# Second-layer logits from seven block products over pairs of token tiles instead of eight

## Chip, core and metric

One core of a Trainium2 chip runs the whole program. The metric is the device time of one execution in microseconds (us); lower is better. TensorE (PE) multiplies matrices, VectorE (DVE), ScalarE (ACT) and GpSimd (POOL) do elementwise work, and SP here only issues transfers. Each engine takes its instructions in the order in which the program holds them.

## The reference

Windowed attention gives 2304 tokens of width 512, and two feed-forward layers follow. The second one is what matters here:

```python
def _moe2_ref(x, w_in, w_out, g_ln):      # x 2304x512, w_in 512x1024, w_out 1024x512
    h = x @ w_in
    h_max = np.max(h, axis=-1, keepdims=True)
    e = np.exp(h - h_max)
    sm = e / (np.sum(e, axis=-1, keepdims=True) + 1e-09)
    solu = h * sm
    mu = np.mean(solu, axis=-1, keepdims=True)
    var = np.mean((solu - mu) ** 2, axis=-1, keepdims=True)
    ln = (solu - mu) / np.sqrt(var + 1e-06) * g_ln
    return (ln @ w_out).astype(np.float32)
```

All data is float32. A float32 product is made of three fast ones: each operand is split into a rounded high part (type fp32r) and the rest, its low part, and high x high, high x low and low x high are added up in PSUM.

## The kernel before

The first part, up to about 523 us, runs attention and the first layer. The first layer goes through six blocks j of 384 tokens; in each block, 16 steps f make a hidden tile (`moe_h`, line 399) and, two steps later, add its product with `w_out` to four accumulators (`moe_y`, line 430). Attention of later tiles is fed in between in small slots. At a block's end `moe_out` copies the accumulators out and POOL sends them to DRAM (`x2d`). In the last block the second layer's weights are loaded, already split (`w2_load`, lines 210 to 217), into the buffers that the first layer's weights leave, and `x2_load`/`x2_split` (lines 549 to 563) load and split the first tokens.

The second layer takes 18 tiles of 128 tokens. For tile i:

- `st_h2` (line 645): 24 matmuls of 128x512 give the logits, 128x1024, in two PSUM banks; there are three such pairs of banks.
- `st_ln` (lines 656 to 668): DVE takes the row maximum, ACT the exponential into a tile `e`, DVE forms the normalised product `s`, ACT its squares, POOL the power -1/2, and DVE the scaled result. `e` and `s` have two buffers.
- `st_move` (lines 679 to 685): the result must be turned around for the next product. DVE transposes 32x32 blocks (into `e`), SP sends the tile to DRAM (`lnd`, one transfer of 512 KB), and, when it has landed, loads it back turned (`lT`, four transfers of 128 KB). The last three tiles (`DIRECT`) are turned on PE instead (line 698).
- `st_t2` (lines 703, 704): ACT makes the high part of `lT` and DVE the low part.
- `st_out` (lines 715 to 722): 24 matmuls of 128x512 give the output tile, ACT copies it, SP sends it to DRAM.

The loop at the end emits `st_h2(i)`, then `st_out(i - 4)`, then the normalisation of tile i, then `st_t2` of tile i - 3, which is pinned behind instructions of the current tile. A scheduler of the build then sets the final order on each engine from its own estimate of times; the order can be read from the built program, and the rows in the section on the change are from there.

Of the kernel before, what the change touches and what calls it, by code (L numbers as in the profile page):

```python
# [20 lines left out]
def kernel(  # L21
# [12 lines left out]
    nc = tc.nc  # L34
# [51 lines left out]
    ps_at = fr_ctx.enter_context(tc.tile_pool(name="ps_at", bufs=2, space=PSUM, side="right"))  # L86
    ps_h = fr_ctx.enter_context(tc.tile_pool(name="ps_h", bufs=2, space=PSUM, side="right"))
    ring = []
    ps_acc = ps_ctx.enter_context(tc.tile_pool(name="ps_acc", bufs=1, space=PSUM))
# [86 lines left out]
    w2ih, w2il, w2oh, w2ol = {}, {}, {}, {}  # L176
    w2d = [dram.tile([128, 1024], F32, name=f"w2d{u}") for u in range(16)]
# [257 lines left out]
    def moe_out(j, es):  # L435
        for e in es:
            xo = wk_p.tile([128, NB], F32, tag="xo", name="xo")
# [109 lines left out]
    x2h, x2l, x2raw = {}, {}, {}  # L547

    def x2_load(j):
        r = d_p.tile([128, KC, NB], F32, tag="x2", bufs=1, name="x2r")  # L550
        nc.sync.dma_start(out=r, in_=x2d[j].rearrange("e p n -> p e n"))
        x2raw[j] = r

    def x2_split(j, es):
        r = x2raw[j]
        if 0 in es:
            x2h[j] = wk_p.tile([128, KC, NB], F32R, tag="xh", name="x2h")
            x2l[j] = wk_p.tile([128, KC, NB], F32R, tag="xl", name="x2l")
        for e in es:
            nc.scalar.copy(x2h[j][:, e, :], r[:, e, :])  # L560
            nc.vector.tensor_tensor(
                x2l[j][:, e, :], r[:, e, :], as_f32(x2h[j][:, e, :]), op=ALU.subtract
            )

# [3 lines left out]
    for n in range(len(seq) + 2):  # L568
# [39 lines left out]
        if n < len(seq):  # L608
# [5 lines left out]
            if last and f >= 2 and f - 2 < 8:  # L614
                w2_load(f - 2, 0)
                w2_load(f - 2, 1)
# [4 lines left out]
        if n < len(seq):  # L621
            if last and 10 <= f < 14:
                x2_split(0, (f - 10,))
            if last and f == 14:
                x2_load(1)
# [4 lines left out]
    ps2 = ctx.enter_context(tc.tile_pool(name="ps2", bufs=2, space=PSUM, reuse_waits="tile"))  # L630
    h2, ln, lnh, lnl = {}, {}, {}, {}
    DIRECT = (NI - 3, NI - 2, NI - 1)
    lnd = [dram.tile([128, DF2], F32, name=f"lnd{i}") for i in range(NI)]

    def st_h2(i):
        j, t = divmod(i, TPN)
        ps = ps2.tile([128, DF2], F32, tag="h2", bufs=3, name="ps_h2")
        tc_ = slice(t * 128, t * 128 + 128)
        for nn in range(2):
            cs = slice(nn * 512, nn * 512 + 512)  # L640
            n = 0
            for kc in range(KC):
                hi, lo = x2h[j][:, kc, tc_], x2l[j][:, kc, tc_]
                for a, w in ((hi, w2ih), (hi, w2il), (lo, w2ih)):
                    nc.tensor.matmul(ps[:, cs], a, w[kc, nn], start=(n == 0), stop=(n == 3 * KC - 1))  # L645
                    n += 1
        h2[i] = ps

    def st_ln(i):
        ps = h2.pop(i)  # L650
        e = d_p.tile([128, DF2], F32, tag="e", name="e")
        s = d_p.tile([128, DF2], F32, tag="s", name="s")
        l_ = s
        st = d_p.tile([128, 8], F32, tag="stat", name="stat")
        nmx, sm, rs, ssum, nmu, vs, rstd = (st[:, z:z + 1] for z in range(7))
        nc.vector.reduce_max(nmx, ps, axis=mybir.AxisListType.X, negate=True)
        nc.scalar.activation(e, ps, ACTF.Exp, bias=nmx, scale=1.0, accum_out=sm)
        nc.vector.tensor_scalar(sm, sm, 1e-9, None, op0=ALU.add)
        nc.vector.reciprocal(rs, sm)  # L659
        nc.vector.scalar_tensor_tensor(s, ps, rs, e, op0=ALU.mult, op1=ALU.mult, accum_out=ssum)  # L660
        nc.vector.tensor_scalar(nmu, ssum, -1.0 / DF2, None, op0=ALU.mult)
        last_act = nc.scalar.activation(e, s, ACTF.Square, bias=nmu, scale=1.0, accum_out=vs).ins
        nc.vector.tensor_scalar(vs, vs, 1.0 / DF2, 1e-6, op0=ALU.mult, op1=ALU.add)
        nc.gpsimd.tensor_tensor(rstd, vs, mhalf, op=ALU.pow)
        if i in DIRECT:
            l_ = e.rearrange("p (k b i) -> p b k i", b=4, i=32)
            s = s.rearrange("p (b k i) -> p b k i", b=4, i=32)
        last_dve = nc.vector.tensor_scalar(l_, s, nmu, rstd, op0=ALU.add, op1=ALU.mult).ins
        ln[i] = l_, e
        return last_act, last_dve  # L670

    def st_move(i):
        l_, lt = ln[i]
        if i not in DIRECT:
            lT = d_p.tile([128, 4, NK2, 32], F32, tag="st", bufs=NST, name="lT")
            nc.vector.transpose(lt, l_)
            nc.sync.dma_start(out=lnd[i], in_=lt)  # L680
            for a in range(4):
                nc.sync.dma_start(
                    out=lT[:, a].rearrange("p k j -> p (k j)"),
                    in_=lnd[i][32 * a:32 * a + 32, :].rearrange("i (b m) -> b i m", b=4),
                )
            ln[i] = lT

    def st_t2(i):
        lnh[i], lnl[i] = {}, {}
        l_ = ln.pop(i)  # L690
        for a in range(2):
            hi, lo = wtile(f"wih{8 + 2 * (i % 2) + a}"), wtile(f"wil{8 + 2 * (i % 2) + a}")
            lnh[i][a], lnl[i][a] = (z.rearrange("p (k t) -> p k t", t=128) for z in (hi, lo))
            if i in DIRECT:
                if a == 0:
                    ps = ps2.tile([128, DF2], F32, tag="h2", bufs=3, name="ps_t2")
                    for c in range(0, DF2, 128):
                        nc.tensor.transpose(ps[:, c:c + 128], l_[1][:, c:c + 128], ident)
                src = ps[:, 512 * a:512 * a + 512]
            else:  # L700
                src = l_[:, :, 4 * a:4 * a + 4, :].rearrange("p a k j -> p k a j")
                hi, lo = (z.rearrange("p (k a j) -> p k a j", k=4, a=4) for z in (hi, lo))
            nc.scalar.copy(hi, src)
            nc.vector.tensor_tensor(lo, src, as_f32(hi), op=ALU.subtract)


    def st_out(i):
        hi, lo = lnh.pop(i), lnl.pop(i)
        w = DM // 2 if i == NI - 1 else DM
        for c in range(0, DM, w):  # L710
            ps = ps2.tile([128, DM], F32, tag="o", name="ps_o")[:, 0:w]
            n = 0
            for kk in range(NK2):
                for a, b in ((hi, w2oh), (hi, w2ol), (lo, w2oh)):
                    nc.tensor.matmul(  # L715
                        ps, a[kk // 4][:, kk % 4, :], b[kk][:, c:c + w],
                        start=(n == 0), stop=(n == 3 * NK2 - 1),
                    )
                    n += 1
            o = d_p.tile([128, DM], F32, tag="o", name="o")[:, 0:w]  # L720
            nc.scalar.copy(o, ps)
            nc.sync.dma_start(out=out[i * 128:(i + 1) * 128, c:c + w], in_=o)

# [4 lines left out]
    pins = []  # L728
    for i in range(NI + LAG):
        if i < NI:  # L730
            st_h2(i)
        if i >= LAG:
            st_out(i - LAG)
        if i - 2 in DIRECT:
            st_t2(i - 2)
        if i < NI:
# [42 lines left out]
```

## Time and profile before

| what | value |
|---|---|
| median of three runs | 736.18 us (734.31 to 736.62) |
| the profiled execution | 734.42 us, of which the span from first to last instruction is 732.6 us |
| mean granted clock of PE in it | 0.990 of full speed |
| busy: PE, DVE, ACT, POOL | 709.4, 416.9, 399.2, 142.3 us |
| first layer's last matmul begins | 522.92 us |
| second layer | from 523.26 us to the end |

A busy time adds up the instructions' own durations. Matmuls are pipelined, so the durations of neighbours overlap; how fast PE goes is read from the distance of the starts. The trace names the instruction that each engine waited for, and the SP queue's timeline shows when a transfer could be issued, which for `lT` is the moment when `lnd` has landed.

### The profile page before, as it was taken

Reading aid. Unit: us, or ns where it says so; the run is one execution under the profiler, and the core shown is the slowest. Engines: PE = TensorE matmul, PEld = TensorE weight load, DVE = VectorE, ACT = ScalarE, POOL = GpSimd, SP = SyncE. Lnnn points to the kernel's source line nnn. Section 1 sums busy time; section 2 is a strip of 40 time slices with the busy share of each in tenths; the row PEclk is TensorE's granted clock in tenths of the full one; section 3 lists DMA queues with packets and bytes.
Section 4 is the critical chain, followed back from the end, with each engine's and each line's share of the span. In section 5 each row is a group of like instructions: output and inputs, shape, how many; then the busy total and the mean of one; then the engine's idle time right before and its main releaser. Section 6 shows DMA issues by size and latency. Waiting matters only on the chain.

```text
span 732.6 us, 12336 instructions
## 1 busy us (share of the span) xinstructions
PE 709.4 (97%) x4321; PEld 649.4 (89%) x4321; DVE 416.9 (57%) x1110; ACT 399.2 (54%) x986; POOL 142.3 (19%) x167
## 2 busy tenths in 40 slices
PE   7799889999999999999999999999999899999998
PEld 5699779999999999999999999999887688888887
DVE  4669987655555665655565543322386547466550
ACT  5878867655565556566665654533344334433441
POOL 2448866201112111211112111100100000000000
PEclk9899999999999999999999999999999899999999
DMA  9996895614245433445332102860233433433221
GB/s 195 219 245 189 220 251 131 155 25 112 78 98 155 119 83 94 124 94 127 88 85 95 55 30 72 282 236 29 87 100 125 150 123 109 156 135 134 97 81 44
DMA packets 152597, 92.05 MB, mean 126 GB/s; under 512 B 117848, under 2 KB 137048, under 8 KB 152536
## 3 DMA queue, kind: packets, MB, share of 16 engines
q1 hardware_dynamic: 143320, 69.76, 36.5%
q0 software_dynamic: 9216, 21.51, 8.7%
q8 instruction: 34, 0.56, 0.3%
q14 instruction: 27, 0.22, 0.1%
HBM read 65.54 MB, written 25.69 MB: 125 GB/s over the span
## 4 chain that ended last, share of the span: by engine, by line
PE 81%; DVE 8%; ACT 4%; DMA 4%; issue 2%; SPq 0%; POOL 0%; DVEq 0%; ACTq 0%; POOLq 0%
PE acc L430 24%; PE ps_h L399 24%; PE ps_o L715 12%; PE ps_h L645 10%; PE ps_s L312 4%; PE ps_x L379 3%; PE ps_p L360 2%; DVE wst L135 2%; DMA lnd<-e 2%; DVE wst L134 1%; ACT p L326 1%; DMA lT<-lnd 1%; DVE s L660 1%; DMA qk<-in_q_dram 1%; PE ps_t L294 1%
## 5 line engine op out<-in xcount | busy, mean ns | idle before, releaser
L399 PE MATMUL ps_h<-xh,wih 128*128 128x384 f32 (+1 forms) x392 | 132.6, 339 | 5.4 <-DVE u L414 5.3
L399 PE MATMUL ps_h<-xl,wih 128*128 128x384 f32 (+1 forms) x392 | 131.5, 336 | 1.1 <-DVE xl L387 1.0
L430 PE MATMUL acc<-gl,woh 128*128 128x384 f32 (+1 forms) x392 | 131.0, 335 | 0.4 <-POOL gl L419 0.4
L399 PE MATMUL ps_h<-xh,wil 128*128 128x384 f32 (+1 forms) x392 | 131.1, 335 | 0.0
L430 PE MATMUL acc<-gh,wol 128*128 128x384 f32 (+1 forms) x392 | 129.9, 333 | 0.0
L430 PE MATMUL acc<-gh,woh 128*128 128x384 f32 (+1 forms) x392 | 126.6, 343 | 0.0
L414 DVE SCALAR_TENSOR_TENSOR u<-u,ps_h 128x384 f32<-128x384 f32 (+1 forms) x98 | 53.4, 544 | 125.8 <-ACT u L409 125.5
L408 ACT ACTIVATE u<-ps_h,half 128x384 f32<-128x384 f32 (+1 forms) x98 | 56.0, 572 | 95.6 <-PE ps_h L399 95.6
L399 PEld LDWEIGHTS ps_h<-xh,wih 128*128 128x128 f32 x392 | 74.5, 190 | 7.3 <-DVE u L414 6.6
L399 PEld LDWEIGHTS ps_h<-xl,wih 128*128 128x128 f32 x392 | 74.6, 190 | 1.6 <-DVE xl L387 1.6
L430 PEld LDWEIGHTS acc<-gl,woh 128*128 128x128 f32 x392 | 73.8, 188 | 1.4 <-POOL gl L419 1.1
L399 PEld LDWEIGHTS ps_h<-xh,wil 128*128 128x128 f32 x392 | 74.5, 190 | 0.0
L430 PEld LDWEIGHTS acc<-gh,wol 128*128 128x128 f32 x392 | 73.7, 188 | 0.1
L415 ACT CAST gh<-u 128x384 fp32r<-128x384 f32 (+1 forms) x98 | 49.6, 507 | 43.5 <-DVE u L414 43.2
L430 PEld LDWEIGHTS acc<-gh,woh 128*128 128x128 f32 x392 | 72.3, 189 | 0.6 <-ACT gh L415 0.2
L144 POOL TENSOR_TENSOR w2st<-wst,w2st 128x512 fp32r<-128x512 f32 x16 | 20.9, 1304 | 229.9 <-ACT w2st L143 169.6
L326 ACT ACTIVATE p<-p,mx 128x128 f32<-128x128 f32 (+1 forms) x144 | 55.8, 390 | 17.5 <-DVE mx L320 17.4
L419 DVE TENSOR_TENSOR gl<-u,gh 128x384 fp32r<-128x384 f32 x80 | 44.6, 557 | 33.0 <-ACT gh L415 32.6
L645 PE MATMUL ps_h<-wih,x2h 128*128 128x512 f32 x144 | 57.1, 396 | 2.8 <-DVE stat L659 2.6
L715 PE MATMUL ps_o<-woh,wih 128*128 128x512 f32 (+1 forms) x152 | 58.6, 385 | 0.0
L715 PE MATMUL ps_o<-wol,wih 128*128 128x512 f32 (+1 forms) x152 | 58.0, 382 | 0.0
L715 PE MATMUL ps_o<-woh,wil 128*128 128x512 f32 (+1 forms) x152 | 57.8, 382 | 0.0
(93 smaller groups left out, 1263.9 us busy)
## 6 DMA issues: line engine op xcount, KB each, us to landing
vw<-in_v_dram SPq DMA_DIRECT2D x32, 256.0 KB
wst<-in_moe_w_in_dram SPq DMA_DIRECT2D x16, 512.0 KB
wst<-in_moe_w_out_dram SPq DMA_DIRECT2D x16, 512.0 KB
w2d<-w2st POOLq DMA_DIRECT2D x16, 512.0 KB, 3.3
lnd<-e SPq DMA_DIRECT2D x15, 512.0 KB
lT<-lnd SPq DMA_DIRECT2D x60, 128.0 KB
x2d<-xo POOLq DMA_DIRECT2D x24, 192.0 KB, 2.2
x2r<-x2d SPq DMA_DIRECT2D x6, 768.0 KB
```

The lines of the kernel that those rows point to most:

```text
L144: nc.gpsimd.tensor_tensor(lo, val, as_f32(hi), op=ALU.subtract)
L312: nc.tensor.matmul(ps[:, i * 128 + c0:i * 128 + 128], qT[g][:, i, :, :].rearrange("p x q -> p (x q)"), kT[g][:, i * 64 + c0:i * 64 + 128], ...
L326: nc.scalar.activation(p[:, i, c0:], tmp[:, i, c0:], ACTF.Exp, bias=mx[:, i:i + 1], scale=-1.0, accum_out=sm[:, i:i + 1],)
L379: nc.tensor.matmul(ps[64 * x:64 * x + 64, i * 64:i * 64 + 64], vw[t, i][0:n, 2 * hp + x, :], o[0:n, i, 64 * x:64 * x + 64], start=True, st ...
L399: nc.tensor.matmul(ps, a, bb[:, kc, c], start=(n == 0), stop=(n == 3 * KC - 1))
L408: nc.scalar.activation(u, ps, ACTF.Relu, bias=half, scale=0.5)
L414: g = nc.vector.scalar_tensor_tensor(u, u, 1.0, ps, op0=ALU.min, op1=ALU.max)
L415: return nc.scalar.copy(hi, u).ins, g.ins
L419: eng.tensor_tensor(lo, u, as_f32(hi), op=ALU.subtract)
L430: nc.tensor.matmul(acc[j, e][:, c], a, bb, start=(f == 0 and n == 0 and c.start == 0), stop=(f == NF - 1 and n == 2),)
L645: nc.tensor.matmul(ps[:, cs], a, w[kc, nn], start=(n == 0), stop=(n == 3 * KC - 1))
L715: nc.tensor.matmul(ps, a[kk // 4][:, kk % 4, :], b[kk][:, c:c + w], start=(n == 0), stop=(n == 3 * NK2 - 1),)
```

## The change

It computes the logits of two token tiles together. The pair's tokens (2x128) and the weights (512x1024) are cut into 2x2 blocks, and Strassen's scheme in Winograd's form makes the four result blocks from seven block products instead of eight. Each product is 6 matmuls of 128x512, so that a pair takes 42 matmuls where two tiles took 48. What goes with it:

- **Weights.** `w2_unit` stores the second layer's first weights unsplit, at half the size (POOL's subtraction of line 144 goes for 8 of its units). In the last block `w2_vals` loads them, `w2_sums` forms four weight sums T1 to T4 (8 subtractions of 128x512 on POOL), and `w2_split` splits 14 tiles (ACT and POOL).
- **Tokens.** `x2_load(p)` loads pair p (512 KB); `x2_prep(p)` forms S1 to S4 (four POOL instructions of 128x256) and splits the seven left operands (four ACT and four DVE instructions, three of 128x512 and one of 128x256).
- **Sums.** ACT copies P1 from PSUM; DVE adds the other products: three plain additions and four with a running maximum, all 128x512 with one operand in PSUM. The maximum of line 656 goes.
- **Order.** Tiles are processed 1, 0, 3, 2 and so on; below they are counted in that order, 0 to 17. Five products of pair 0 stand in steps 8, 9, 10, 12 and 14 of the last block, P2 and P3 of it at the block's end.
- **Buffers and queues.** Six single banks of PSUM for products, three `e` and `s`, four `lT` for five; the output goes out on ACT's queue, no longer on SP's; two `DIRECT` tiles for three.

```diff
@@ weights @@
+                if u < 8:
+                    z = stage["p"].tile([128, 512], F32, tag="st", bufs=NST, name="w2st")
+                    nc.scalar.copy(z, st[:, :, 1].bitcast(F32))
+                    nc.gpsimd.dma_start(out=w2d[u], in_=z)
+                    continue
...
+    def w2_sums(k):
...
+        for y, a, b in (("T1", "B12", "B11"), ("T2", "B22", "T1"), ("T3", "B22", "B12"), ("T4", "B21", "T2")):
+            nc.gpsimd.tensor_tensor(w2v[y, k], w2v[a, k], w2v[b, k], op=ALU.subtract)
+
+    def w2_split(n):
+        v_ = w2v.pop(WORDER[n])
+        hi, lo = w2h[WORDER[n]], w2l[WORDER[n]] = wtile(f"wih{n}"), wtile(f"wil{n}")
+        nc.scalar.copy(hi, v_)
+        nc.gpsimd.tensor_tensor(lo, v_, as_f32(hi), op=ALU.subtract)
@@ second layer @@
+    def x2_load(p):
+        r = x2r[p] = d_p.tile([128, KC, 256], F32, tag="x2", bufs=2, name="x2r")
...
+    def x2_prep(p):
...
+        for o, a, b, op in ((s1, a21, a22, add), (s2, s1, a11, sub), (s3, a11, a21, sub), (s4, a12, s2, sub)):
+            nc.gpsimd.tensor_tensor(o, a, b, op=op)
...
+        for (hi, src), (lo, _) in zip(part["xh"], part["xl"]):
+            nc.scalar.copy(hi, src)
+            nc.vector.tensor_tensor(lo, src, as_f32(hi), op=ALU.subtract)
...
+    def prod(p, y, a, w):
+        ps = p_bank(y)
+        n = 0
+        for k in range(2):
+            hi, lo = x2h[p][a][:, k, :], x2l[p][a][:, k, :]
+            for l, r in ((hi, w2h[w, k]), (hi, w2l[w, k]), (lo, w2h[w, k])):
+                nc.tensor.matmul(ps, l, r, start=(n == 0), stop=(n == 5))
+                n += 1
+        return ps
...
+        if y == "P1":
+            nc.scalar.copy(u[1], prod(p, y, "A11", "B11"))
+        elif y == "P6":
+            add(u[2], prod(p, y, "S2", "T2"), u[1])
+        elif y == "P7":
+            add(u[3], prod(p, y, "S3", "T3"), u[2])
+        elif y == "P5":
+            ps = prod(p, y, "S1", "T1")
+            add_max(s[:, 512:], ps, u[3], m1)
+            add(u[4], ps, u[2])
+        elif y == "P4":
+            add_max(s[:, :512], prod(p, y, "A22", "T4"), u[3], m0)
+        elif y == "P2":
+            add_max(s[:, :512], prod(p, y, "A12", "B21"), u[1], m0)
+        else:
+            add_max(s[:, 512:], prod(p, y, "S4", "B22"), u[4], m1)
...
-        nc.vector.reduce_max(nmx, ps, axis=mybir.AxisListType.X, negate=True)
...
-            nc.sync.dma_start(out=out[i * 128:(i + 1) * 128, c:c + w], in_=o)
+            nc.scalar.dma_start(out=out[i * 128:(i + 1) * 128, c:c + w], in_=o)
...
+    P_STEPS = {8: "P1", 9: "P6", 10: "P7", 12: "P5", 14: "P4"}
...
-    for i in range(NI + LAG):
-        if i < NI:
-            st_h2(i)
-        if i >= LAG:
-            st_out(i - LAG)
+    for m in range(2, NI + LAG):
+        p = m // 2
+        if m < NI:
+            for y in PARTS[m % 2]:
+                st_p(m, y)
+        if m >= LAG:
+            st_out(m - LAG)
...
+            if m % 2 == 0 and p + 2 < NI // 2:
+                x2_load(p + 2)
+            if m % 2 == 0 and p + 1 < NI // 2:
+                with tc.issue_after(ln_pins[m - 1][0]), tc.issue_after(ln_pins[m - 1][1]):
+                    x2_prep(p + 1)
```

Three places show how the order on the engines moves. The first is PE where the first output tile begins (`ps_o` is an output tile, `ps_h2` the logits of a tile, P1 to P7 products). Before:

```order
L645 MATMUL ps_h2_6643<-wih5_5909,x2h_6461 128x512
L645 MATMUL ps_h2_6643<-wil5_5910,x2h_6461 128x512
L645 MATMUL ps_h2_6643<-wih5_5909,x2l_6462 128x512
L715 MATMUL ps_o_6500<-woh0_5708,wih8_6467 128x512
L715 MATMUL ps_o_6500<-wol0_5709,wih8_6467 128x512
L645 MATMUL ps_h2_6643<-wih7_5991,x2h_6461 128x512
L645 MATMUL ps_h2_6643<-wil7_5992,x2h_6461 128x512
L645 MATMUL ps_h2_6643<-wih7_5991,x2l_6462 128x512
L715 MATMUL ps_o_6585<-woh0_5708,wih10_6552 128x512
L715 MATMUL ps_o_6585<-wol0_5709,wih10_6552 128x512
```

Changed:

```order
L631 MATMUL P3_6540<-wih13_6335,x2p_6372 128x512
L631 MATMUL P1_6580<-wih0_5735,x2p_6510 128x512
L631 MATMUL P1_6580<-wil0_5736,x2p_6510 128x512
L631 MATMUL P6_6588<-wih2_5823,x2p_6510 128x512
L631 MATMUL P6_6588<-wil2_5824,x2p_6510 128x512
L631 MATMUL P7_6596<-wih4_5923,x2p_6510 128x512
L631 MATMUL P7_6596<-wil4_5924,x2p_6510 128x512
L746 MATMUL ps_o_6622<-woh0_5739,woh8_6522 128x512
L746 MATMUL ps_o_6622<-wol0_5740,woh8_6522 128x512
L631 MATMUL P1_6580<-wih0_5735,x2p_6512 128x512
L631 MATMUL P1_6580<-wih1_5782,x2p_6510 128x512
```

Before, seven tiles of logits (0 to 6) stand ahead of or around the first output. Changed, it comes after all products of pair 0 and pair 1 and six matmuls of pair 2.

The second is the SP queue in the second layer (`x2r` loads tokens, `out` is the output). Before, around tiles 7 to 9:

```order
L680 DMA lnd7_6258<-e_6783 128x1024
L682 DMA lT_6796<-lnd7_6258 128x1x256 x4
L551 DMA x2r_7143<-x2d5_65 128x4x384
L722 DMA out_0_dram<-o_6865 128x512
L680 DMA lnd8_6259<-e_6868 128x1024
L682 DMA lT_6881<-lnd8_6259 128x1x256 x4
L722 DMA out_0_dram<-o_6948 128x512
L680 DMA lnd9_6260<-e_6951 128x1024
L682 DMA lT_6964<-lnd9_6260 128x1x256 x4
```

Changed, from the second processed tile on (lnd0) to the fifth (lnd5):

```order
L586 DMA x2r_6667<-x2d2_62 128x4x128
L586 DMA x2r_6667<-x2d3_63 128x4x128
L712 DMA lnd0_539<-e_6391 128x1024
L714 DMA lT_6401<-lnd0_539 128x1x256 x4
L712 DMA lnd3_542<-e_6485 128x1024
L714 DMA lT_6495<-lnd3_542 128x1x256 x4
L586 DMA x2r_6853<-x2d3_63 128x4x256
L712 DMA lnd2_541<-e_6549 128x1024
L714 DMA lT_6559<-lnd2_541 128x1x256 x4
L712 DMA lnd5_544<-e_6650 128x1024
L714 DMA lT_6660<-lnd5_544 128x1x256 x4
```

The output has left the queue; the token loads stand ahead of the `lnd` of the pair's second tile.

The third is DVE, where the low part of a loaded tile (`wil` or `wol` out of `lT`) meets the transposition of a later one. Before:

```order
L668 TENSOR_SCALAR s_6697<-s_6697,stat_6698 128x1024
L704 TENSOR_TENSOR wil8_6808<-lT_6541,wih8_6807 128x512
L704 TENSOR_TENSOR wil9_6812<-lT_6541,wih9_6811 128x512
L679 STREAM_TRANSPOSE e_6696<-s_6697 128x1024
L656 TENSOR_REDUCE stat_6785<-ps_h2_6730 128x1
```

Changed, at processed tiles 1 and 2:

```order
L692 TENSOR_SCALAR stat_6531<-stat_6531 128x1
L699 TENSOR_SCALAR s_6441<-s_6441,stat_6442 128x1024
L734 TENSOR_TENSOR wol10_6567<-lT_6401,woh10_6566 128x512
L734 TENSOR_TENSOR wol11_6571<-lT_6401,woh11_6570 128x512
L711 STREAM_TRANSPOSE e_6485<-s_6441 128x1024
```

In both, the transposition stands behind the low part. Here, before, it is tile 6 behind tile 4; in the changed kernel tile 2 stands behind tile 1, and from tile 4 on a tile stands behind the one two before it.

## Rows read from the trace of the kernel before

**Rows 1.** the page: busy us (share of the span) and instructions by engine.

```profile
PE 709.4 (97%) x4321; PEld 649.4 (89%) x4321; DVE 416.9 (57%) x1110; ACT 399.2 (54%) x986; POOL 142.3 (19%) x167
```

**Rows 2.** chain that ended last, second layer: start us, us, what.

```profile
516.81 6.46 PE acc L430 x36
523.26 11.17 PE ps_h L645 x48
...
633.63 5.44 PE ps_o L715 x24
...
704.36 0.87 PE ps_t L698 x8
...
717.91 11.22 PE ps_o L715 x72
```

**Rows 3.** a stage: stretch, length, busy us by engine, PEclk, DMA share, GB/s.

```profile
600.00:650.00 50.00, 50.00 (x222) 41.41 (x221) 31.63 (x60) 21.77 (x41) 2.74 (x5) 1.00 0.41 137
```

**Rows 4.** timeline of PE: start us, us, instruction, idle before, releaser.

```profile
77.45 0.45 PE L399 MATMUL ps_h<-xh,wih 128*128 128x384 f32 x1 [1.71 <-DVE u L414]
...
575.86 0.77 PE L645 MATMUL ps_h<-wih,x2h 128*128 128x512 f32 x1 [2.61 <-DVE stat L659]
...
581.95 0.44 PE L715 MATMUL ps_o<-woh,wih 128*128 128x512 f32 x1
```

**Rows 5.** timeline of the SP queue (it issues the transfers), second layer.

```profile
538.55 0.32 SPq L680 DMA_DIRECT2D lnd<-e  x1
541.28 2.29 SPq L682 DMA_DIRECT2D lT<-lnd  x4
...
547.54 0.33 SPq L680 DMA_DIRECT2D lnd<-e  x1
553.23 2.17 SPq L682 DMA_DIRECT2D lT<-lnd  x4
...
562.89 2.20 SPq L682 DMA_DIRECT2D lT<-lnd  x4
...
573.03 2.17 SPq L682 DMA_DIRECT2D lT<-lnd  x4
...
616.76 2.18 SPq L682 DMA_DIRECT2D lT<-lnd  x4
619.18 0.37 SPq L551 DMA_DIRECT2D x2r<-x2d  x1
...
629.64 2.18 SPq L682 DMA_DIRECT2D lT<-lnd  x4
...
640.15 2.28 SPq L682 DMA_DIRECT2D lT<-lnd  x4
...
650.77 2.18 SPq L682 DMA_DIRECT2D lT<-lnd  x4
```

**Rows 6.** timeline of ACT: first reads of a loaded tile lT.

```profile
638.51 1.14 ACT L703 CAST wih<-lT 128x512 fp32r<-128x512 f32 x2 [3.92 <-DMA lT<-lnd]
...
649.08 0.62 ACT L703 CAST wih<-lT 128x512 fp32r<-128x512 f32 x1 [1.37 <-DMA lT<-lnd]
```

**Rows 7.** 553 to 563 us in 40 slices: tenths of 16 DMA engines busy.

```profile
DMA  0000002222222499997221122221222222212000
```

**Rows 8.** DVE by line and form: count, busy us, mean ns, idle before.

```profile
L320 DVE CUSTOM_DVE_ANT_0 p<-ps_s,mask 128x128 f32<-128x128 f32 x128 | 30.8, 286 | 15.4 <-PE ps_s L312 15.3
...
L660 DVE SCALAR_TENSOR_TENSOR s<-ps_h,stat,e 128x1024 f32<-128x1024 f32 x18 | 23.1, 1284 | 0.6
...
L704 DVE TENSOR_TENSOR wil<-lT,wih 128x512 fp32r<-128x512 f32 x30 | 19.5, 688 | 14.3 <-ACT wih L703 14.0 <-PE ps_o L715 0.3
L679 DVE STREAM_TRANSPOSE e<-s 128x1024 f32<-128x1024 f32 x15 | 18.6, 1238 | 0.0
```

**Rows 9.** timeline of DVE: line 134 beside a busy POOL, and alone.

```profile
59.36 1.07 DVE L134 TENSOR_SCALAR wst<-wst 128x512 uint32<-128x512 uint32 x1
...
442.88 0.42 DVE L134 TENSOR_SCALAR wst<-wst 128x512 uint32<-128x512 uint32 x1
```

More of the change, by code (lines that the diff above doesn't have):

```diff
@@ L172, in w1_unit @@
         return w_unit(src, hi, lo)
-    w2ih, w2il, w2oh, w2ol = {}, {}, {}, {}
-    w2d = [dram.tile([128, 1024], F32, name=f"w2d{u}") for u in range(16)]
+    w2h, w2l, w2oh, w2ol = {}, {}, {}, {}
+    w2d = [dram.tile([128, 512 if u < 8 else 1024], F32, name=f"w2d{u}") for u in range(16)]
     def w2_unit(n, which):
@@ L436, in moe_out @@
         for e in es:
-            xo = wk_p.tile([128, NB], F32, tag="xo", name="xo")
+            xo = wk_p.tile([128, NB], F32, tag="u" if j == NBLK - 1 and e > 1 else "xo", name="xo")
             a = acc.pop((j, e))[:, 0:NB]
@@ L546 @@
     NI = NT // 128
[L547 to L562, printed above, removed]
-            )
+    x2r, x2h, x2l = {}, {}, {}
@@ new lines, with p_bank @@
+    pb, h2, ln, lnh, lnl = {}, {}, {}, {}, {}
+    ORDER = [2 * p + 1 - z for p in range(NI // 2) for z in range(2)]
+    DIRECT = ORDER[-2:]
+    lnd = [dram.tile([128, DF2], F32, name=f"lnd{i}") for i in range(NI)]
+    def p_bank(name):
+        if ps2:
+            return ps2[0].tile([128, 512], F32, tag="p", bufs=6, name=name)
+        return ring[0].tile([128, 512], F32, tag="r", name=name)
+    def prod(p, y, a, w):
[7 more added lines that the diff above has]
+        return ps
@@ new lines, in st_move @@
+    def st_move(m):
+        l_, lt = ln[m]
+        i = ORDER[m]
+        if i not in DIRECT:
+            lT = d_p.tile([128, 4, NK2, 32], F32, tag="st", bufs=4, name="lT")
+            nc.vector.transpose(lt, l_)
+            nc.sync.dma_start(out=lnd[i], in_=lt)
+            for a in range(4):
+                nc.sync.dma_start(
+                    out=lT[:, a].rearrange("p k j -> p (k j)"),
+                    in_=lnd[i][32 * a:32 * a + 32, :].rearrange("i (b m) -> b i m", b=4),
+                )
+            ln[m] = lT
@@ new lines, in st_out @@
+    def st_out(m):
+        hi, lo = lnh.pop(m), lnl.pop(m)
+        i = ORDER[m]
+        w = DM // 2 if m == NI - 1 else DM
+        for c in range(0, DM, w):
+            ps = ps2[0].tile([128, DM], F32, tag="o", bufs=2, name="ps_o")[:, 0:w]
+            n = 0
+            for kk in range(NK2):
+                for a, b in ((hi, w2oh), (hi, w2ol), (lo, w2oh)):
+                    nc.tensor.matmul(
+                        ps, a[kk // 4][:, kk % 4, :], b[kk][:, c:c + w],
+                        start=(n == 0), stop=(n == 3 * NK2 - 1),
+                    )
+                    n += 1
+            o = d_p.tile([128, DM], F32, tag="o", name="o")[:, 0:w]
+            nc.scalar.copy(o, ps)
+            nc.scalar.dma_start(out=out[i * 128:(i + 1) * 128, c:c + w], in_=o)
@@ L613 @@
             w2_step(n, *pins)
-            if last and f >= 2 and f - 2 < 8:
-                w2_load(f - 2, 0)
-                w2_load(f - 2, 1)
+            if last and f < 2:
+                w2_vals(f)
+            if last and f in (2, 3):
+                w2_sums(f - 2)
+            if last and f >= 2:
+                with tc.issue_after(pins[0]):
+                    w2_split(f - 2)
+            if last and 2 <= f < 10:
+                w2_load(f - 2)
         else:
@@ L621 @@
         if n < len(seq):
-            if last and 10 <= f < 14:
-                x2_split(0, (f - 10,))
-            if last and f == 14:
-                x2_load(1)
+            if last and f == 1:
+                x2_load(1)
+            if last and f == 5:
+                with tc.issue_after(pins[0]), tc.issue_after(pins[1]):
+                    x2_prep(0)
+            if last and f in P_STEPS:
+                st_p(0, P_STEPS[f])
+            if last and f == 14:
+                l2_norm(0)
@@ L628 @@
+            if last and f == 15:
+                st_p(1, "P2")
+        elif n == len(seq):
+            x2_load(2)
+            x2_prep(1)
+            st_p(1, "P3")
+            l2_norm(1)
     assert next(stages, 0) == 0
     ps_ctx.close()
[L630 to L647, printed above, removed]
@@ L675, in st_move @@
[L675 to L686, printed above, removed]
@@ L688, in st_t2 @@
[L688 to L704, printed above, removed]
@@ L707, in st_out @@
[L707 to L721, printed above, removed]
-            nc.sync.dma_start(out=out[i * 128:(i + 1) * 128, c:c + w], in_=o)
```

157 lines of the change are left out of this document (113 added, 44 removed).

## Prediction

> **What bounds the kernel now.** I begin with the page: PE is busy 97% of the span [rows 1], so either PE's work or something that PE waits for sets the end. The chain that ended last is PE without a break through the end of the first layer and the beginning of the second, and again after an interruption to the end [rows 2]. In steady state 24 matmuls of 128x512 take 5.44 us, 0.2267 us each; a tile costs 10.88 us, logits and output [rows 2, 3]. So PE paces the second layer, with one interruption: a wait of 2.61 us before 575.86, after which fourteen matmuls take from there to 581.95, 6.09 us in place of 3.17, before their starts come at the old distance again. Wait and slow stretch together cost 5.5 us [rows 4].
>
> The second thing to read is who is nearly late. The SP queue sends `lnd`, waits until it has landed, issues four `lT`, and begins again. Undisturbed, `lnd` lands 2.73 us after its issue (538.55 to 541.28). Behind a fresh `lT` it takes far longer, and the distance from one `lT` issue to the next becomes a cycle: 9.66 us (553.23 to 562.89) and 10.14 (to 573.03) where nothing else passes the queue, 10.51 and 10.62 (629.64, 640.15, 650.77) with an output in each, 12.88 (616.76 to 629.64) where a token load of 768 KB stands in it too [rows 5]. ACT's first read of the tile comes 6.7 us after the last of the four issues (631.82 to 638.51; 642.43 to 649.08) [rows 5, 6], so a tile is back 8.8 us after its first `lT` issue. While only `lT` runs, the 16 engines are two tenths busy, with one burst of nine tenths in between [rows 7]: the load is slow because few engines carry it, and `lnd`'s share on those same engines comes behind it. This cycle, 10.6 us, is hardly shorter than PE's tile of 10.88 us. The chain names PE only because PE needs a little more.
>
> The Trainium skill, page "DMA: Bandwidth & Descriptors", section "Why a DMA increments its semaphore by 16 and not by 1", says how many engines a transfer gets: as many, up to 16, as divide the slowest dimension of both its sides. For `lT`, whose source begins with a dimension of 4, that is 4 engines of 16, and the two tenths agree [rows 7]. By the same page, section "Issuing engines are not separate DMA queues", moving a transfer to another engine's queue brings it no more engines; by it the output's bytes would stay in the cycle, the cycle would stay near 10.62 us, and the sum below would come to about 740 us.
>
> **What PE gains.** Nine pairs at 42 for 48 matmuls: 54 x 0.2267 = 12.24 us less. One tile fewer is turned on PE: 0.87 us [rows 2]. If the wait and the slow stretch go too, 5.5 us. By PE alone the end would come 18.6 us earlier.
>
> **What the first layer's end pays.** 42 products stand within the last block, so that PE leaves it 42 x 0.2267 = 9.52 us later, at 532.8 us. POOL's 22 new instructions of 128x512 and the tokens' sums lie beside some 67 us of the block (16 steps of 24 matmuls at 6.46/36 us [rows 2]); POOL is busy 142 us of the whole span [rows 1]. I take them as hidden, and ACT's splits also. If a split came late, its product would wait in front of the block's own matmuls, us for us. The 8 subtractions that vanish from earlier blocks lay off PE's path: nothing.
>
> **What the transfers do then.** Now the first outputs need their tiles much sooner: before, some seven tiles of logits stood ahead of the first output, now two pairs and six matmuls, as the order shows. So the transfer cycle has no head start. Step by step, tiles in processing order:
> - Tile 0's sums end in the block; its transposition needs about 7 us of DVE and ACT behind P4 and the block's gates, and it is back about 11 us after P3's end, 543.9 us, when PE has done pair 1 (532.8 + 9.52 + 6 matmuls = 543.7). No wait worth a term.
> - Tile 1: after P3 at 532.8, DVE's order up to its transposition holds five sums with a maximum or without (P3, P6, P7, P5 twice), P4, the normalised product, a scaling, four splits for pair 2 and the small ones: 12.4 us at the durations of [rows 8], with one exponential waited for. `lnd` at 545.3; with the token load ahead of it 3.6 us (between 2.73 and the 5.69 of 547.54 to 553.23 [rows 5]); `lT` at 548.9, back at 557.7.
> - Tile 2's transposition stands behind the low part of tile 1: ACT and DVE 1.9 us, transposition 1.24 [rows 8], `lnd` undisturbed 2.73 [rows 5]: `lT` at 563.5, back at 572.3.
> - Tile 3 follows on the queue, with a token load ahead: `lT` at 574.4.
> - From here the queue is never idle: 12 cycles to tile 15. The token loads of three later pairs add 1.5 us each (12.88 less 10.62 is 2.26 for 768 KB; these are 512 KB [rows 5]): 4.5 us. For the cycle I take 10.14 us, the longer of the bare two and the middle between 9.66 and 10.62, since the output leaves the queue but not the engines. 574.4 + 4.5 + 121.7 = 700.6; back at 709.4.
> - Then ACT's first half 0.6 us, output 15 with its wait for the low part and the last transpositions 6.6, outputs 16 and 17 as 5.44 and 5.5 [rows 2]: PE ends at 727.5. Before it ended at 717.91 + 11.22 = 729.13 [rows 2]. The copy and transfer behind it stay.
>
> **The sum** is 1.6 us less: a span of 731.0 for 732.6, 732.8 us for the profiled execution's 734.42. That execution lies 1.76 us below the median of the three runs; put on the median, 734.6 us. About 17 of PE's 18.6 us come back as waits for `lT`. PE would end pair and output work at 710.5 if no tile were late.
>
> Bounds: with 9.66 us for every cycle 5.8 us less, 728.8; if tiles 1 to 3 also follow at that cycle (DVE's order costing nothing), another 5 us less, 724. With 10.62, 5.8 more, 740.4, and with token loads at the full 2.26, 742.7.
>
> **DVE's load** is the cost that the trace doesn't show directly. A product's sum, 128x512 from PSUM, lies between 0.688 us (line 704, same size, SBUF) and, scaling line 320's 0.286 for 128 columns fourfold, 1.14; I take 0.69 plain and 0.77 with a maximum, since the same line's cost per column, and not its start, grows. Two tiles of before take DVE 31.63/50 x 21.76 = 13.8 us [rows 3]. The change adds seven sums (four plain, three with a maximum, 5.1 us) and more token splits (four low parts of 512 columns at about the 0.69 of line 704, for some 1.5 us before: 1.2 more), and takes away two separate maxima over 1024 columns, which I put at the transposition's 1.24 each, the same size [rows 8]: 13.8 + 5.1 + 1.2 - 2.5 = 17.6 of PE's 20.4 us per pair (42 matmuls and two outputs). It fits, without much room.
>
> **Rivals.**
> - *Transfers don't bind.* For it: the output leaves SP, three `e` buffers, four `lT`. Against it: even the shortest cycle, 9.66, plus half a token load is longer than PE's mean of 9.5 us between outputs 1 and 15 (14 outputs and some six pairs in 133 us). Its best is the bound above, 724 us.
> - *DVE sets the pace (slower).* DVE waits in its own order for the exponential, the square, POOL's power and `lT`. If it needs more than the transfers' two cycles and a token load, 21.8 us per pair, each us above that costs 7 us over seven pairs. With 4.2 us of uncovered waits on 17.6 nothing happens; with 5.2 it is 741.6 us. POOL now works beside it: line 134 took 1.07 us beside a busy POOL and 0.42 alone [rows 9], so four token sums a pair can stretch DVE by one or two us. The Trainium skill, page "SBUF — State Buffer", section "Who interferes with whom", says that GpSimd and VectorE exclude each other on one pair of ports, a DVE operation with two SBUF inputs among them; rows 9 agree in kind.
> - *The waits slow PE.* A wait of 1.71 us left the distance of the starts as it was, one of 2.61 us doubled it for 6 us [rows 4]. If each odd tile's output waits over 2 us, PE's pair grows from 20.4 by 2.9 us and PE itself becomes late: about 740 us.
> - *The change doesn't do what it says:* products in the last block wait for POOL's splits, 3 to 8 us for the block, and no later gain: about 739 us.
>
> **How the numbers follow.** Forecast, transfers bind: 0.55, own range 728 to 741, of which a little over two fifths lies more than 0.3% (2.2 us, about what a measurement of this kernel can tell from no change) below the median before, a third within it. Transfers don't bind: 0.19, faster. DVE or a slowed PE: 0.21, slower. Late splits: 0.05, slower. Faster 0.24 + 0.19 = 0.43; same 0.20; slower 0.11 + 0.21 + 0.05 = 0.37. Range: 724 to 742.5 us.
>
> **What would show it.** Right: 378 matmuls at line 631 for the 432 at line 645, at the same 0.2267 us; on SP `lT` issues from tile 3 on 9.7 to 10.6 us apart, 11 to 12 with a token load, and `lnd` never waiting for DVE there; PE waiting for `lT`'s first half before outputs 1, 3 and above all 14 and 15. Wrong: SP waiting for DVE between `lnd`s (DVE sets the pace); no wait of PE at all (transfers don't bind, some 720 us); gaps in the last block before P1 to P4 (late splits); a PEclk of 0.5 in many slices.

## The result, and the profile after

The changed kernel takes 743.92 us (median of four runs, 743.21 to 744.77) for 735.96 before (four runs here): 1.0118 times as long, with a 95% interval of 1.0103 to 1.0133. The profiled execution took 744.17 us, its span is 742.4. The forecast was 734.6 us with a range up to 742.5: wrong in the direction, and the measured time lies 1.4 us outside the range.

One caution on single executions. Up to 79 us the instructions of every engine stand in the same order in all the kernels of this document. Yet the same long wait of PE (line 399 before, 429 after) ends at 77.45 us in the profiled execution of before [rows 4], at 78.87 in that of the changed kernel, and between 77.23 (e5) and 79.34 us (e3) in those below. Times of two profiled executions therefore compare to within 2 us only; distances taken behind that point compare better.

The page shows that PE did less work and ended later, as an answer to [rows 1]; below it are the waits of PE from 540 us on (engine, line, what it waited for, total us, times, longest):

```profile
PE 702.7 (95%) x4259; PEld 639.4 (86%) x4259; DVE 456.7 (62%) x1222; ACT 418.3 (56%) x1021; POOL 190.1 (26%) x217
...
PE ps_o L746 <- ACT woh L733: 8.0, 5, 4.1
PE ps_o L746 <- DVE wol L734: 7.1, 4, 4.2
PE P L631 <- ACT u L665: 1.4, 2, 1.2
PE ps_o L746 <- ACT o L752: 1.1, 1, 1.1
PE ps_t L729 <- DVE e L699: 0.3, 1, 0.3
```

Together 17.9 us of waits, 15.1 of them at outputs, for the high or the low part of a tile that has come back through DRAM. Before, [rows 2] showed PE with one interruption. The SP queue, as [rows 5] (a start of `lT` is the moment when `lnd` has landed), from tile 0 on:

```profile
541.20 2.27 SPq L714 DMA_DIRECT2D lT<-lnd  x4
...
551.19 0.33 SPq L712 DMA_DIRECT2D lnd<-e  x1
554.32 2.18 SPq L714 DMA_DIRECT2D lT<-lnd  x4
...
569.38 2.29 SPq L714 DMA_DIRECT2D lT<-lnd  x4
571.78 0.48 SPq L586 DMA_DIRECT2D x2r<-x2d  x1
573.89 0.33 SPq L712 DMA_DIRECT2D lnd<-e  x1
581.51 2.17 SPq L714 DMA_DIRECT2D lT<-lnd  x4
587.17 0.32 SPq L712 DMA_DIRECT2D lnd<-e  x1
590.81 2.24 SPq L714 DMA_DIRECT2D lT<-lnd  x4
...
700.46 2.42 SPq L714 DMA_DIRECT2D lT<-lnd  x4
...
710.76 2.17 SPq L714 DMA_DIRECT2D lT<-lnd  x4
```

The last tile's `lT` begins at 710.76 us; the forecast had 700.6. From tile 3 to tile 15 it is 129.25 us, 10.77 per cycle. The cycles alternate: after 581.51 SP is free at 583.7 and waits until 587.17 for DVE before the next `lnd`, which then lands in 3.6 us; the other `lnd` of a pair goes out at once and needs 7.6 us behind a fresh `lT`. That an `lnd` waits for DVE is what the prediction had named as the sign of another case (DVE sets the pace). So two readings stood against each other: **TRANSFERS** (the way through DRAM is at its limit whatever DVE does) and **ORDER** (DVE waits for something, and that delays every second tile). For ORDER spoke these rows of DVE by line and form (count, busy us, mean ns, idle before):

```profile
L660 DVE CUSTOM_DVE_ANT_0 s<-P,u 128x512 f32<-128x512 f32 x35 | 23.5, 681 | 0.3
...
L657 DVE TENSOR_TENSOR u<-P,u 128x512 f32<-128x512 f32 x24 | 16.4, 684 | 13.5 <-ACT u L665 13.3
L699 DVE TENSOR_SCALAR s<-s,stat 128x1024 f32<-128x1024 f32 x16 | 13.4, 836 | 23.4 <-POOL stat L695 23.4
```

DVE's sums cost 0.68 us each, near the forecast (0.69, and 0.77 with a maximum). But the scaling at line 699 waits 23.4 us in all for POOL's power, which stands on POOL behind the four token sums of a later pair, and these wait for the token load.

### The profile page after: what moved, and what is told of

It reads as the page before. It is cut to its first block, busy times and chain, and to the rows that moved or that the text cites. A ratio compares the mean times of both kernels' runs of the same rounds, so it can differ in the third digit from the quotient of the medians.

```text
span 742.4 us, 12389 instructions
## 1 busy us (share of the span) xinstructions
PE 702.7 (95%) x4259; PEld 639.4 (86%) x4259; DVE 456.7 (62%) x1222; ACT 418.3 (56%) x1021; POOL 190.1 (26%) x217
## 3 DMA queue, kind: packets, MB, share of 16 engines
q1 hardware_dynamic: 143272, 64.00, 33.8%
## 5 line engine op out<-in xcount | busy, mean ns | idle before, releaser
L449 DVE TENSOR_TENSOR gl<-u,gh 128x384 fp32r<-128x384 f32 x80 | 54.7, 684 | 35.1 <-ACT gh L445 34.7
L631 PE MATMUL P<-wih,x2p 128*128 128x512 f32 x216 | 71.1, 392 | 1.9 <-ACT u L665 1.4
L746 PE MATMUL ps_o<-woh,woh 128*128 128x512 f32 (+1 forms) x152 | 59.2, 390 | 9.1 <-ACT woh L733 8.0
L746 PE MATMUL ps_o<-woh,wol 128*128 128x512 f32 (+1 forms) x152 | 59.6, 392 | 7.1 <-DVE wol L734 7.1
L746 PE MATMUL ps_o<-wol,woh 128*128 128x512 f32 (+1 forms) x152 | 58.7, 386 | 0.0
L439 ACT ACTIVATE u<-u 128x384 f32<-128x384 f32 (+1 forms) x98 | 51.0, 520 | 2.3
```

The source lines that it names most:

```text
L439: nc.scalar.activation(u, u, ACTF.Square)
L449: eng.tensor_tensor(lo, u, as_f32(hi), op=ALU.subtract)
L631: nc.tensor.matmul(ps, l, r, start=(n == 0), stop=(n == 5))
L746: nc.tensor.matmul(ps, a[kk // 4][:, kk % 4, :], b[kk][:, c:c + w], start=(n == 0), stop=(n == 3 * NK2 - 1),)
```

## Experiments

**e1: another shape for `lT`.** The source of `lT` was, for each of four quarters, 4 x 32 rows; with the partitions in the order (i, b) in place of (b, i) it is 128 rows, and the four transfers become one. The rows of the last weights and of g_ln follow that order.

```diff
-            for a in range(4):
-                nc.sync.dma_start(
-                    out=lT[:, a].rearrange("p k j -> p (k j)"),
-                    in_=lnd[i][32 * a:32 * a + 32, :].rearrange("i (b m) -> b i m", b=4),
-                )
+            nc.sync.dma_start(
+                out=lT.rearrange("p a k j -> p a (k j)"),
+                in_=lnd[i].rearrange("(a i) (b m) -> (i b) a m", a=4, b=4),
+            )
...
-        src = w_out2.rearrange("(b k i) m -> k b i m", b=4, i=32)[n]
+        src = w_out2.rearrange("(b k i) m -> k i b m", b=4, i=32)[n]
...
-            l_ = e.rearrange("p (k b i) -> p b k i", b=4, i=32)
+            l_ = e.rearrange("p (k i b) -> p b k i", b=4, i=32)
```

> The changed kernel with lT loaded by one transfer of 128 rows of 4x1 KB instead of four transfers whose source begins with a dimension of 4 (the partition order of the second layer's last weights follows). Two theories. TRANSFERS: the way of a tile through DRAM, 8.7 us from the first lT issue to ACT's read, holds everything in the second layer. Then the 18.4 us of PE's waits and most of the slow clock behind the two of over 4 us go: 722 to 728 us for 743.9, lT issues free of the pattern 9.3/12.2 us, PE waiting less than 4 us in the second layer. ORDER: what holds is DVE's wait for POOL's power behind the token sums (22.9 us in nine waits); the token load lands some us sooner too since less stands before it, but the sums still stand ahead: 738 to 741 us, with DVE still waiting over 12 us for line 695.

Measured: 717.81 us, 0.9759 of the kernel before (0.9745 to 0.9774), even below what TRANSFERS expected. The load of 512 KB lands 3.9 us after its issue, and the engines show why. First the changed kernel, 10 us from 599.3 us on in 40 slices (tenths of the 16 DMA engines busy), then e1, the same stretch, with its row of issues (count, KB, median us to landing):

```profile
DMA  2122222222120000000312112122222222222222
```

```profile
DMA  8000079967999999998699838899930000000000
...
lT<-lnd SPq DMA_DIRECT2D x2, 512.0 KB, 3.9
```

Two tenths busy for the whole length of a load, as in [rows 7], against nine tenths for a short one (the row of e1 holds an `lnd`, two token loads and an output besides). The pages count 143272 packets on SP's hardware queue in both kernels, so it isn't that there are fewer of them. With the short load the waits of PE in the second layer are gone: from 450 us on the view of waits lists only two gaps in the last block and one of 0.5 us at its end:

```profile
PE acc L460 <- DVE gl L449: 1.5, 2, 0.9
PE P L631 <- DVE xo L472: 0.5, 1, 0.5
```

A stage of e1 (columns as [rows 3]) has PE busy throughout and DVE 86% busy:

```profile
600.00:650.00 50.00, 50.00 (x222) 41.40 (x221) 43.12 (x99) 26.48 (x48) 10.59 (x13) 1.00 0.47 164
```

Of the distance between the two profiled spans (742.4 and 715.9 us) 1.5 us isn't the load's: line 429's wait ends at 77.35 us in e1 and at 78.87 in the changed kernel, in the same order of instructions.

**e5: the shape alone.** Four transfers as in the changed kernel, each with 128 rows.

```diff
-                    in_=lnd[i][32 * a:32 * a + 32, :].rearrange("i (b m) -> b i m", b=4),
+                    in_=lnd[i][32 * a:32 * a + 32, :].rearrange("i (b m) -> (i b) m", b=4),
```

> Between the changed kernel and e1 two things differ: one issue instead of four, and a source of 128 rows instead of one that begins with a dimension of 4. Here only the second: four transfers of 128 KB for a tile as in the changed kernel, each with a source of 128 rows. SHAPE (the four-row source makes the load slow): within 3 us of e1, 717 to 721 us, since the 1.6 us more of issuing per tile have room. ISSUES (the four issues on one queue cost the time): 735 to 744 us.

Measured: 719.33 us (0.9775). What counts is the shape, not the number of issues. The rule that the prediction cited from the Trainium skill ("DMA: Bandwidth & Descriptors", "Why a DMA increments its semaphore by 16 and not by 1": as many engines, up to 16, as divide the slowest dimension of both sides) says just this, and e1 and e5 agree.

**e2: ORDER alone.** Only the place of POOL's token sums is moved, from pair 3 on (`pows` collects line 695's instructions).

```diff
-            nc.gpsimd.tensor_tensor(o, a, b, op=op)
+            with tc.issue_after(pows[2 * p - 5]) if p > 2 else ExitStack():
+                nc.gpsimd.tensor_tensor(o, a, b, op=op)
```

> The changed kernel with one thing moved: POOL's token sums of a pair are put behind the powers of the two tiles that they delayed, instead of ahead of them. Nothing is added or removed. ORDER: DVE's waits for POOL's power (22.9 us in nine) go to under 5 us, every second transposition is 3 to 5 us earlier, and so is its lnd; over six pairs 12 us or more: 732 us or less. TRANSFERS: lnd comes earlier, but then finds the previous lT still running, as the other lnd of the pair does now (8.0 us to land for 3.6): the pair shrinks from 21.5 us towards two bare cycles of 10.14, by 0.5 to 1.2 us: 736.5 to 741 us.

Measured: 743.57 us, no change. DVE's wait for the power did go (waits of DVE from 540 to 720 us, here line 701 is the scaling and 697 the power; before the edit 22.9 us in nine). Its place is taken by waits for the high part of the loaded tile, that is, for `lT` (19.0 us, 3.7 before the edit). SP's `lnd` goes out right behind `lT` or a token load, yet the next `lT` comes no earlier:

```profile
DVE wol L736 <- ACT woh L735: 19.0, 7, 5.4
...
DVE s L701 <- POOL stat L697: 4.2, 7, 0.7
```

```profile
582.91 2.17 SPq L716 DMA_DIRECT2D lT<-lnd  x4
585.18 0.53 SPq L714 DMA_DIRECT2D lnd<-e  x1
592.59 2.35 SPq L716 DMA_DIRECT2D lT<-lnd  x4
...
711.76 2.17 SPq L716 DMA_DIRECT2D lT<-lnd  x4
```

From tile 3 to tile 15 it is 128.85 us, for 129.25. The wait on DVE had cost nothing: what `lnd` lost before its issue it won behind it. ORDER falls, as cause of the loss. TRANSFERS had its number wrong too: it expected a pair to shrink by 0.5 to 1.2 us and 736.5 to 741 us, and a pair stayed at 21.5 us.

**e4: the kernel before with e1's load.** Its edit is that of e1.

> The kernel before with the same lT load as in e1, nothing else. TRANSFERS: before, the way through DRAM took part in one wait (2.61 us for an e buffer that lnd held) and the slow clock behind it, 5.5 us together; PE's work sets the rest, so 729 to 733 us for 736, and not less. ORDER says nothing else here. Against e1 it prices the scheme with the way through DRAM out of the question: PE's 12.24 + 0.87 us less the last block's gaps of 1.5 us if nothing else is late, so e1 10 to 13 us below e4; if something else is late, less.

Measured: 728.55 us (0.9903, 0.9887 to 0.992), just under what was expected and 7.1 us less than the 735.63 of the kernel before. The profiled spans lie only 5.6 us apart (732.6 and 727.0), but e4's long wait of line 399 ends at 78.70 us, 1.25 later than that of before. From the first layer's last matmul to PE's end it is 206.19 us before (522.92 to 729.12) and 199.45 in e4 (524.21 to 723.66), 6.7 less. So the load was worth about 7 us already in the kernel before, more than the 5.5 us that the prediction read in the interruption [rows 4]. With the load out of the way the scheme itself saves 728.55 - 717.81 = 10.74 us by the medians (9.7 between the profiled executions, counted from the end of that wait). PE's work is 12.24 + 0.87 = 13.11 us less; about 2 us go to three gaps around the end of the last block (below).

**e3: half the tiles past DRAM.** `DIRECT = ORDER[1::2] + ORDER[-2:-1]` for `ORDER[-2:]`.

> The changed kernel with the second tile of every pair turned on PE (as the last two already are) instead of through DRAM. PE gets eight tiles x 0.87 us = 7.0 us more work, the way through DRAM carries eight tiles for sixteen. TRANSFERS: PE without late tiles would end at about 712 (710.5 and 1.5 us of gaps in the last block), so 719 with the added work, and no wait is left: 721 to 727 us. ORDER: DVE still waits for the power in each pair, and the tiles behind it: 734 to 742 us.

Measured: 729.02 us (0.991), 2 us above what TRANSFERS expected and far below ORDER's. PE's waits in the second layer are 3.1 us in three, where the estimate had none. With 7.0 us more work on PE it is 15 us faster.

**e6: an earlier start.** Three orders at the beginning of the second layer (`turns` holds line 711's instructions).

```diff
-            x2_prep(1)
+            with tc.issue_after(ln_pins[0][0]), tc.issue_after(turns[0]):
+                x2_prep(1)
...
-                with tc.issue_after(ln_pins[m - 1][0]), tc.issue_after(ln_pins[m - 1][1]):
+                with tc.issue_after(ln_pins[m - 1][0]), tc.issue_after(turns[m - 1] if m == 2 else ln_pins[m - 1][1]):
                     x2_prep(p + 1)
...
-                with tc.issue_after(act), tc.issue_after(dve):
+                with tc.issue_after(act), tc.issue_after(turns[z + 1] if z == 1 else dve):
                     st_t2(z)
```

> The changed kernel, slow lT as it is, with three orders set at the start of the second layer alone: the splits of pair 1's tokens behind tile 0's transposition, those of pair 2's behind tile 1's, and tile 1's low part behind tile 2's transposition. OFFSET (the queue is at its limit from tile 3 on, so what the first tiles lose is never made up): the lT issue of tile 3, 581.5 us in the changed kernel, comes 5 to 8 us earlier and the end comes earlier by as much: 736 to 739 us. FORGOTTEN (the later tiles are held by something else, DVE's order, PE's slow clock, so that the start does not matter): 742 to 745 us.

Measured: 737.9 us, 6.0 below the changed kernel. SP's rows of tiles 3 and 15:

```profile
577.04 2.18 SPq L715 DMA_DIRECT2D lT<-lnd  x4
...
706.00 2.17 SPq L715 DMA_DIRECT2D lT<-lnd  x4
```

4.5 us earlier at tile 3, where 5 to 8 were expected, and 4.8 at tile 15; another 1.5 us come behind tile 15. Of the 4.5 us, 1.6 are there before the edit acts, at the first layer's last matmul (534.08 us for 535.67); the three orders give 2.9. Whichever its cause, a late start is not made up.

**e7: the output on SP's queue again.** `nc.sync.dma_start` for `nc.scalar.dma_start` at line 753.

> One part of the change undone: the output goes out on SP's queue again instead of ACT's. If leaving the queue was worth what the prediction took (about half a us per cycle of lT, 10.14 for 10.62): 749 to 752 us. If the bytes of the output use the same engines whichever queue they come from, and the cycle did not gain by it: 742 to 746 us.

Measured: 744.67 us for 743.92, the same within the intervals, and 130.24 us from tile 3's `lT` to tile 15's for 129.25, where the prediction had counted half a us per cycle, 6 us. Which queue issues the output hardly matters.

**e10: the output's bytes.** `out[..., c:c + 32]` from `o[:, 0:32]` at line 753.

> The changed kernel with the slow lT, but only the first 32 of 512 columns of every output tile are sent to DRAM (the rest is left out). It prices the output's bytes. If they take their share of the few engines that carry lT, a cycle shrinks by some of the 0.5 to 1 us by which 10.62 lies above 9.66 and 10.14: 733 to 739 us. If they do not lie in its way: 742 to 744.5 us.

Measured: 737.75 us, 6.2 below the changed kernel. SP's rows of tiles 3 and 15, 125.0 us apart for 129.25:

```profile
580.41 2.17 SPq L714 DMA_DIRECT2D lT<-lnd  x4
...
705.42 2.17 SPq L714 DMA_DIRECT2D lT<-lnd  x4
```

The bytes lie in the way. Together with e7 this agrees with the rule that the prediction had cited in a sentence by itself (the Trainium skill, "DMA: Bandwidth & Descriptors", "Issuing engines are not separate DMA queues").

**e9: three tiles turned on PE.** `DIRECT = ORDER[-3:]`.

> One part of the change undone: three tiles turned on PE again instead of two, so that the way through DRAM carries 15 tiles, as in the kernel before. PE gets 0.87 us more. If the last tile through DRAM sets the end, it comes a cycle (10.7 us) earlier but with one more output of 5.44 us behind it: 4.4 us less, 739.5 us; if PE's order before tile 14's output sets it, as the wait of 4.15 us before 712.95 us suggests, only 0.5 to 2 us less: 742 to 743.5 us.

Measured: 745.66 us, 1.7 above the changed kernel: both readings missed. PE's last long wait is for tile 14 there too. Its `lT` starts at 701.21 us, but ACT makes the high part only behind the exponential and the square of tile 16, and DVE the low part behind its scaling. ACT's rows of e9:

```profile
707.94 1.15 ACT L688 ACTIVATE e<-s,stat 128x1024 f32<-128x1024 f32 x1 [5.63 <-DVE stat L681]
...
711.18 1.15 ACT L693 ACTIVATE e<-s,stat 128x1024 f32<-128x1024 f32 x1 [1.53 <-DVE stat L692]
...
712.33 1.12 ACT L733 CAST woh<-lT 128x512 fp32r<-128x512 f32 x2
```

Its output begins at 712.98 us, for 712.95 in the changed kernel, waits once more for the low part (1.09 us), and has 0.87 us more of transpositions behind it. The way is shorter by a tile, and that does not help, since it was not tile 15 that came last.

**e8: e1 without tiles turned on PE.** `DIRECT = ()`.

> e1 with no tile turned on PE: the last two go through DRAM too. In e1 PE was without a gap from the end of the first layer, so its 16 transpositions (2 x 0.87 us) come off the end, if tile 17 is back before PE is at its output (normalised at 692.8 us in e1, output 17 begins about 707 us): 715.5 to 716.7 us. If it is not back in time, above 717.8 us.

Measured: 715.91 us, 0.9722 of the kernel before (0.9701 to 0.9742), the fastest here.

## Why the prediction was wrong, point by point

**What bounds before** was read rightly: PE, with the way through DRAM close behind. The price of the second was read too low: 5.5 us, where e4 has about 7. Between 575.86 us and 581.95 the trace has thirteen matmuls, not fourteen, so that the interruption alone is 5.75 us.

**What PE gains** was right: 54 matmuls and a tile's transpositions fewer. "PE would end pair and output work at 710.5" if no tile were late, and in e1, with the waits gone, it ended at 712.6, the difference being the three gaps of 2 us.

**That the transfers bind and give it back** was right, and e1, e2 and e5 show it. What failed is the sum: the step-by-step times of the first tiles, and after them the length of the cycle. Against the profiled executions it lacks 11.4 us (732.8 forecast, 744.17 measured). By `lT`'s starts and PE's end, which the chain puts at 739.1 us:

| step of the prediction | forecast | measured | more than the step before |
|---|---|---|---|
| tile 1: `lT` | 548.9 | 554.32 | 5.4 |
| tile 3: `lT` | 574.4 | 581.51 | 1.7 |
| tile 15: `lT` | 700.6 | 710.76 | 3.1 |
| PE's end | 727.5 | 739.1 | 1.4 |

- **The first tiles, 5.4 us.** This is the step that failed most, though 1.4 us of it are not the change's: this execution was that much later at 78 us already (above). The prediction took the first layer's end as the old one plus 9.52 us, with POOL's and ACT's additions hidden. 1.5 us are two gaps in the last block, of 0.67 and 0.87 us, where PE waited for DVE's line 449; its rows stand in the last section. The rest, some 2.5 us, is in the order of ACT and DVE. Tile 0's square stands on ACT behind the splits of pair 1, and these wait for POOL's token sums:

```profile
530.48 0.62 ACT L612 CAST x2p<-xs 128x512 fp32r<-128x512 f32 x1 [1.30 <-POOL xs L600]
531.64 0.63 ACT L612 CAST x2p<-xs 128x512 fp32r<-128x512 f32 x1 [0.53 <-POOL xs L600]
...
533.10 1.15 ACT L693 ACTIVATE e<-s,stat 128x1024 f32<-128x1024 f32 x1
```

So tile 0's transposition came 11.1 us after P4's sum began (525.52 to 536.59 us), where "about 7 us of DVE and ACT" were forecast, and it stood in front of tile 1's sum. "No wait worth a term" was wrong twice: PE waited 1.81 us for tile 0, and what was late at tile 0 was late ever after. e6, which sets this and two more orders at the start, ends 6.0 us earlier by the medians and has 2.9 us of it at tile 3.

- **The cycles, 3.1 us.** 10.14 us and 1.5 per token load were taken, on the ground that the output leaves the queue. The changed kernel had 129.25 us and e2, whose queue is hardly idle, 128.85 us for the forecast 126.2. The output's bytes stayed on the same engines; e7 and e10 show that this, and not the queue, counts. With a sixteenth of the bytes e10 has 125.0 us, close to the forecast: in effect the prediction had taken them out together with the queue. The end of 10.62 us, which it kept for the range, gives 131.9 us, so that the measured time lies about midway.

- **The tail, 1.4 us.** Forecast was an end set by tile 15. In the changed kernel, as in e9, PE's last long wait was for tile 14. Its `lT` had begun at 700.46 us, but ACT reached its high part only at 712.29, behind tile 16's exponential and square:

```profile
712.95 0.53 PE L746 MATMUL ps_o<-woh,woh 128*128 128x512 f32 x1 [4.15 <-ACT woh L733]
713.28 0.62 PE L746 MATMUL ps_o<-wol,woh 128*128 128x512 f32 x1
...
715.37 0.63 PE L746 MATMUL ps_o<-woh,woh 128*128 128x512 f32 x1
715.79 0.63 PE L746 MATMUL ps_o<-wol,woh 128*128 128x512 f32 x1
...
717.14 0.39 PE L746 MATMUL ps_o<-woh,wol 128*128 128x512 f32 x1
717.37 0.39 PE L746 MATMUL ps_o<-woh,woh 128*128 128x512 f32 x1
```

Behind it the starts are 0.42 us apart for some 4 us and then 0.23 again; the granted clock is 0.50, that is 1.2 GHz, between 714.4 and 716.6 us. After the other long wait, 4.17 us before 630.74, the same is seen.

**The rivals.** *Transfers don't bind*: no, 717.81 us in e1 is what that would have given. *DVE sets the pace*: its sign was there (SP waiting for DVE), and its reasoning named POOL's power, but e2 shows that the wait was covered. DVE's load in e1, 43.12 of 50 us, is the 17.6 of 20.4 us that the prediction worked out (it counted four plain sums and three with a maximum where the code has three and four, 0.08 us at its prices). *The waits slow PE*: it happens, after two waits of over 4 us; in e1 both the waits and the slowing are gone, so it came on top of them and was no cause of its own. Its price doesn't follow either: by the rule that the prediction used for DVE, a pair of 20.4 + 2.9 us would end near 745 us, not 740; but only two waits at outputs were over 2 us. Nor does the length of one wait decide, as [rows 4] may suggest: in e2 a wait of 3.16 us before 638.87 left the starts 0.23 us apart (granted clock 1.00 from 639.2 to 643 us), and one of 1.95 us before 592.17 was followed by starts 0.43 us apart (0.50 from 594 to 596.4). *Late splits*: no product waited in the block; the block lost its 1.5 us in another way.

**The range** ended at 742.5 us because only the cycle had been given a longer side; the steps of tiles 0 to 3, added up from durations with hardly a wait, had been given only a shorter one ("another 5 us less"). What stays open: of the 25 us by which PE was later than in e1 after the first layer, 17.9 are waits of the table; the starts at the lower clock, some twelve of them 0.2 us late each, come to about 2.5 us (an estimate from the starts in the trace); the small gaps that make up the rest were not added up.

## What to carry to other kernels

A resource that keeps up by a hair (10.6 us of 10.88) is the bound as soon as the one in front of it gets faster; before a faster scheme is costed, that second one must be mended. Here it was one access pattern, worth 7.1 us in the kernel before and 26.1 us in the changed one, where the scheme itself gives 10.7. Where a chain of transfers never rests, its first link counts in full: the order of the engines at the start, waits on other engines included, has to be worked through there with a longer as well as a shorter side. Two kernels are compared from a point behind which they differ: here single executions were up to 2 us apart before the change began. A wait of an engine, however long in the table, is only a cause if taking it away moves the end.

## What the runs showed of the hardware

An operation of DVE with two operands in SBUF was held up here for as long as POOL worked almost without a break. In the last block POOL forms the weight sums; DVE's and POOL's rows of that time:

```profile
458.25 1.07 DVE L449 TENSOR_TENSOR gl<-u,gh 128x384 fp32r<-128x384 f32 x1 [0.58 <-ACT gh L445]
...
462.75 5.39 DVE L449 TENSOR_TENSOR gl<-u,gh 128x384 fp32r<-128x384 f32 x1 [0.58 <-ACT gh L445]
...
469.18 0.56 DVE L449 TENSOR_TENSOR gl<-u,gh 128x384 fp32r<-128x384 f32 x1 [0.58 <-ACT gh L445]
```

```profile
462.11 1.29 POOL L241 TENSOR_TENSOR w2t<-w2v 128x512 f32<-128x512 f32 x1
463.34 0.57 POOL L473 DMA_DIRECT2D x2d<-xo  x1
463.93 1.30 POOL L241 TENSOR_TENSOR w2t<-w2v,w2t 128x512 f32<-128x512 f32 x1
465.18 2.53 POOL L241 TENSOR_TENSOR w2t<-w2v 128x512 f32<-128x512 f32 x2
```

The same instruction takes 0.56 us and 5.39 us; it begins when POOL's subtraction of 462.11 is under way and ends (468.14) just after POOL's row of subtractions (467.71). PE waited for it 0.67 us. In [rows 9] the price of POOL beside DVE had been 0.65 us for a single instruction, there of one operand. That the two exclude each other is in the Trainium skill ("SBUF — State Buffer", "Who interferes with whom"); how long one of them can be shut out was not foreseen. No run here moved these subtractions, so the link to them rests on the rows: all ten profiled kernels with the new weights have such an instruction of 5.38 or 5.39 us in the last block and one of 4.90 to 4.95, while before and in e4, where POOL is almost idle then, the same subtraction (line 419) takes 0.56 us at most from 425 us on.
